# Performer attention with a feed-forward block on one core: the weights' low bits by a 16-bit ScalarE write, and own banks for each half of the first key chunk

## The chip, the core and the metric

The kernel runs on one NeuronCore of a Trainium2 chip: TensorE (PE) for matrix products, VectorE (DVE), ScalarE (ACT), GpSimd (POOL), and SyncE (SP), whose queue issues nearly all transfers. Each engine works through its own instructions in the order in which they were written; an instruction that has to wait holds up all behind it on that engine. PE writes to PSUM, which has eight banks of 512 fp32 values for each of the 128 partitions.

The metric is the device time of one execution in microseconds (us). Before the change three runs gave 965.83, 966.06 and 967.17 us: the median is 966.06 us.

## What is computed

```python
def phi(x):                       # x: (8, 8, 576, 64), omega: (128, 64)
    h = einsum('bhsd,md->bhsm', x, omega) - sum(x * x, -1) / 2
    return exp(h - max(h, -1)) / sqrt(m)
q_p, k_p = phi(q * scale), phi(k * scale)
kv, z = einsum('bhsm,bhsd->bhmd', k_p, v), sum(k_p, axis=2)
num, den = einsum('bhsm,bhmd->bhsd', q_p, kv), einsum('bhsm,bhm->bhs', q_p, z)
x = (num / (den + 1e-6)) as (8, 576, 512)
xn = (x - mean(x)) / sqrt(var(x) + 1e-6) * g_ln
out = x + relu(xn @ w_ch1) @ w_ch2          # 512 -> 2048 -> 512
```

The weights `w_ch1`, `w_ch2` and the vector `g_ln` come as 64-bit floats, the rest as 32-bit.

## The kernel before

**Tiles.** The 8·576 = 4608 rows are cut into 36 chunks of 128, four of them to a tile of 512: nine tiles. The feed-forward block takes a tile through 16 parts f of the hidden layer. Part f of the first layer (`mm1`, L1041 to L1043) is 12 matmuls of 128x512: four slices of the inner dimension, each as high·high, low·high and high·low halves of values that are split in two. Part f of the second layer (`mm2`, L1082 to L1084) is 12 more. Between them `relu` empties the bank: ScalarE writes the high half (L1055), VectorE the low half (L1057).

**Attention** runs between these parts, as visits of PE: keys of a chunk against omega (`gen_k`, L638; the first chunk L629), sums over keys and values (`gen_sums`, L701), queries against omega (`gen_q`, L799; later ones L816, L817), and the quotient's two sides for a chunk (`gen_x`, L882). For keys VectorE takes the negated row maximum (L641) and ScalarE the exponential (L647). For queries a copy leaves PSUM, POOL's all-reduce takes a maximum over partitions (L828), VectorE subtracts it (L833) and ScalarE exponentiates (L836). `gen_x` divides on VectorE (L889, L891, L893, which makes x). A normalised copy xn (L966) is transposed: for the first tile by PE (L1011), ScalarE's copy (L1015) and VectorE's remainder (L1017); for later tiles by a transposing DMA (`gen_flip`): ScalarE splits into 16-bit halves (L983), SP issues (L986), and ScalarE (L354) or VectorE (L356) puts the halves together.

**The first matmuls of the feed-forward block** need x of the first two chunks, so the first tile's keys, values and queries all come ahead of them. Up to then dummy matmuls on a tile named `spin` (L474) fill PE. Eight banks stand for this stage; three pairs of them (0 to 5) are handed out to keys and queries. The first key chunk is worked in two halves (`gen_k_half`, L654): both write into one pair of banks and into columns of one tile of maxima, `mb`, and the pair is given back when both halves are exponentiated.

**Weights** (`gen_w`, L501) come in 32 parts of 512 KB, 64-bit values as pairs of 32-bit words: `r[:, :, 0]` the low word, `r[:, :, 1]` the high word. A part is made into one fp32 value by integer work: the sign bit, the high word scaled as an fp32 number by 2^-112 and shifted left by three, and the upper three bits of the low word below that. Then it is split into a high and a low half (`w[:, 0]`, L354 or L356; `w[:, 1]`, L555 or L549). There are two ways up to the shift: with ScalarE first (L515: low word times 2^-29, written as a 32-bit integer; L517 on VectorE ors in the sign; L360 or L362 scales), or with VectorE first (L523 sign, L527 shift and or). Thirty parts go the first way, two the second. L531 shifts and ors.

**What sets the order.** All instructions are written out by a planner (`Plan`) that keeps its own clock for each engine, takes the ready step with the smallest rank, and knows constants for queues and transfers. `SHIFT` (L1176) is a table that moves the rank of single steps. Different constants and shifts give another order on every engine.

Of the kernel before, what the change touches and what calls it, by code (L numbers as in the profile page):

```python
# [308 lines left out]
def favor_ffn(ctx, tc, kT, kTr, vF, vR, qT, qD, omT, gT, w1, w2, out):  # L309
# [48 lines left out]
    def scaled(eng, out, in_, c):  # L358
        if eng == ACT:
            nc.scalar.activation(out=out, in_=in_, func=AF.Copy, scale=c)  # L360
        else:
            nc.vector.tensor_scalar(out=out, in0=in_, scalar1=c, scalar2=None, op0=ALU.mult)  # L362
# [138 lines left out]
    def gen_w(n, f):  # L501
# [6 lines left out]
            yield wait(*BEFORE)  # L508
        w_turn = yield "get", turn["w"]
        wt = yield "get", n_big  # L510
        eng = yield either(0.58, 0.34)
        t = tile_of(wt, [P, DM], U32)
        sign = 0x80000000
        if eng == ACT:
            nc.scalar.activation(out=t, in_=r[:, :, 0], func=AF.Copy, scale=2.0**-29 * 7.49 / 8)  # L515
            yield dve2(DM)
            nc.vector.scalar_tensor_tensor(  # L517
                out=r[:, :, 0], in0=r[:, :, 1], scalar=sign, in1=t, op0=ALU.bitwise_and, op1=ALU.bitwise_or
            )
            eng = yield either(0.58, 0.34)  # L520
            scaled(eng, f32(r[:, :, 1]), f32(r[:, :, 1]), 2.0**-112)
        else:
            nc.vector.tensor_scalar(out=t, in0=r[:, :, 1], scalar1=sign, scalar2=None, op0=ALU.bitwise_and)  # L523
            eng = yield either(0.58, 0.34)
            scaled(eng, f32(r[:, :, 1]), f32(r[:, :, 1]), 2.0**-112)
            yield dve2(DM)
            nc.vector.scalar_tensor_tensor(  # L527
                out=r[:, :, 0], in0=r[:, :, 0], scalar=29, in1=t, op0=ALU.logical_shift_right, op1=ALU.bitwise_or
            )
        yield dve2(DM)  # L530
        nc.vector.scalar_tensor_tensor(  # L531
            out=t, in0=r[:, :, 1], scalar=3, in1=r[:, :, 0], op0=ALU.logical_shift_left, op1=ALU.bitwise_or
        )
# [66 lines left out]
    def gen_k(b, c, kraw, early, owners, t_v, n_kp, last):  # L600
# [17 lines left out]
        yield wait("om")  # L618

        if not last:  # L620
            t_b = yield "pair", pairs_now()
            pk = two(t_b).rearrange("p s (a b) -> p s a b", b=M)
            left_k = [0, 1]
            for i in range(2):
                yield "run", {PE: 0.5}, 0.03
                for p in range(2 * i, 2 * i + 2):
                    for h in range(2):
                        a = slice(h * D, (h + 1) * D)
                        nc.tensor.matmul(pk[:, h, p], kraw[a, p], om[a], start=True, stop=True)  # L629
# [21 lines left out]
        free(t_mb)  # L651
        done(("kp", b, c))

    def gen_k_half(b, c, i, pk, mb, kp, left_k, t_b, t_mb):  # L654
        cols = slice(2 * i, 2 * i + 2)
        yield dve(4 * M)
        nc.vector.tensor_reduce(
            out=mb.rearrange("p (s a) -> p s a", s=2)[:, :, cols], in_=pk[:, :, cols], axis=AX.X, op=ALU.max, negate=True
        )
        yield us(ACT, 1.0)  # L660
        for s in range(2):
            for p in range(cols.start, cols.stop):
                j = slot(2 * p + s)
                nc.scalar.activation(
                    out=kp[:, j], in_=pk[:, s, p], func=AF.Exp, scale=1.0, bias=mb[:, j : j + 1]
                )
# [312 lines left out]
    def gen_flip(t, i, xn, t_n, xn_turn):  # L979
# [3 lines left out]
        nc.scalar.copy(out=halves, in_=xn.bitcast(U16).rearrange("p (a b) -> p b a", b=2))  # L983
# [252 lines left out]
```

## Time and profile before

| | |
|---|---|
| median of three runs | 966.06 us |
| the profiled execution's own time | 967.0 us |
| its span, first to last instruction | 965.2 us |
| around the span | 1.8 us |
| granted TensorE clock, mean | 1.000 |
| DVE busy | 450.9 us (47%) |
| ACT busy | 406.4 us (42%) |
| POOL busy | 120.4 us (12%) |
| first `mm1` matmul | 34.56 us after the span's start |
| dummy matmuls | 47 |
| moved by DMA | 91.45 MB, 29.6% of 16 engines' span |

Times in the profile are counted from the span's start. A row of the timeline has the start, the length, engine, line, operation, what it writes and reads, and in brackets how long the engine had been idle and what ended that. Matmuls overlap each other, so a row's length is longer than the distance from one start to the next; work on PE, VectorE and ScalarE is counted here by distances between starts. A row of the waits has the total, the number and the longest.

### The profile page before, as it was taken

How to read it: one execution, taken by the hardware profiler on the slowest of the kernel's cores; microseconds unless marked ns; L12 is line 12 of the kernel's file. 1: busy time of each engine (PE TensorE's matmuls, PEld its weight loads, DVE VectorE, ACT ScalarE, POOL GpSimd, SP SyncE). 2: the span in 40 equal slices, each digit the busy share in tenths (PEclk: the TensorE clock that was granted, in tenths of full speed). 3: DMA queues.
4: the chain of work that ended last, by engine and by line, in shares of the span. 5: the costliest groups of instructions: out<-in, count | busy, mean ns of one | idle time of the engine just before them, and what ended most of it. 6: DMA issues, size and time to landing. Idle time of an engine off the chain costs nothing.

```text
span 965.2 us, 15982 instructions
## 1 busy us (share of the span) xinstructions
PE 955.8 (99%) x6731; PEld 787.2 (82%) x6731; DVE 450.9 (47%) x787; ACT 406.4 (42%) x753; POOL 120.4 (12%) x47
## 2 busy tenths in 40 slices
PE   8999999999999999999999999999999999999998
PEld 6877778788888888888888888788888888888886
DVE  6999976245534574344553254535342131113112
ACT  6899874265344543445363234554232121101010
POOL 5012104021010140113011040032010000000000
PEclk9999999999999999999999999999999999999999
DMA  8676364224343243324250213322212020002001
GB/s 299 232 262 229 132 175 124 86 88 131 67 133 98 70 124 104 89 77 100 77 161 16 88 56 91 106 67 77 77 45 77 1 98 1 1 1 87 1 1 44
DMA packets 70584, 91.45 MB, mean 95 GB/s; under 512 B 38000, under 2 KB 38384, under 8 KB 70512
## 3 DMA queue, kind: packets, MB, share of 16 engines
q1 hardware_dynamic: 70368, 90.17, 29.6%
q8 instruction: 53, 0.87, 0.4%
q10 hardware_dynamic: 144, 0.26, 0.1%
q14 instruction: 19, 0.16, 0.1%
HBM read 63.15 MB, written 18.87 MB: 85 GB/s over the span
## 4 chain that ended last, share of the span: by engine, by line
PE 52%; ACT 1%; DMA 1%; DVE 0%; issue 0%; DVEq 0%; ACTq 0%
PE b L1082 8%; PE b L1041 8%; PE b L1084 8%; PE b L1043 8%; PE b L1083 8%; PE b L1042 8%; PE b L882 1%; PE b L701 1%; PE b L638 1%; PE b L816 1%; PE b L817 1%; DMA wide<-wide 1%; ACT wide L354 0%; DVE x L893 0%; ACT quad L809 0%
## 5 line engine op out<-in xcount | busy, mean ns | idle before, releaser
L1057 DVE SCALAR_TENSOR_TENSOR hid<-b,hid 128x512 fp32r<-128x512 f32 x144 | 99.3, 690 | 341.1 <-ACT hid L1055 340.6
L1082 PE MATMUL b<-w,hid 128*128 128x512 f32 x577 | 228.8, 396 | 1.1 <-ACT hid L1055 1.1
L1041 PE MATMUL b<-xnT,w 128*128 128x512 f32 (+1 forms) x584 | 227.0, 389 | 0.7 <-ACT kp L647 0.7
L1042 PE MATMUL b<-xnT,w 128*128 128x512 f32 (+1 forms) x584 | 225.7, 386 | 0.0
L1043 PE MATMUL b<-xnT,w 128*128 128x512 f32 (+1 forms) x584 | 225.6, 386 | 0.0
L1084 PE MATMUL b<-w,hid 128*128 128x512 f32 x577 | 224.8, 390 | 0.0
L1083 PE MATMUL b<-w,hid 128*128 128x512 f32 x577 | 224.6, 389 | 0.0
L1055 ACT ACTIVATE hid<-b 128x512 fp32r<-128x512 f32 x144 | 86.3, 599 | 319.7 <-PE b L1043 319.4
L828 POOL PARTITION_ALL_REDUCE quad<-quad x34 | 114.2, 3388 | 595.5 <-ACT quad L354 360.1
L1082 PEld LDWEIGHTS b<-w,hid 128*128 128x128 f32 x577 | 108.2, 188 | 27.3 <-ACT hid L1055 1.5
L1041 PEld LDWEIGHTS b<-xnT,w 128*128 128x128 f32 x584 | 109.7, 188 | 24.2 <-ACT kp L647 1.7
L1043 PEld LDWEIGHTS b<-xnT,w 128*128 128x128 f32 x584 | 109.7, 188 | 22.3
L1084 PEld LDWEIGHTS b<-w,hid 128*128 128x128 f32 x577 | 108.4, 188 | 23.8 <-DVE hid L1057 0.7
L1042 PEld LDWEIGHTS b<-xnT,w 128*128 128x128 f32 x584 | 109.7, 188 | 22.1 <-DVE w L555 0.4
L1083 PEld LDWEIGHTS b<-w,hid 128*128 128x128 f32 x577 | 108.4, 188 | 21.4
L647 ACT ACTIVATE kp<-b,mb 128x128 f32<-128x128 f32 x256 | 70.1, 395 | 29.6 <-DVE mb L641 29.6
L966 ACT ACTIVATE wide<-x,st 128x512 f32<-128x512 f32 x30 | 21.7, 723 | 84.7 <-DVE x L893 74.5
L833 DVE TENSOR_TENSOR quad<-quad,quad 128x1024 f32<-128x1024 f32 x34 | 53.3, 1575 | 3.5 <-POOL quad L828 3.5
L641 DVE TENSOR_REDUCE mb<-b 128x8 f32<-128x1024 f32 x35 | 41.5, 1218 | 18.0 <-PE b L638 17.5
L836 ACT ACTIVATE quad<-quad 128x1024 f32<-128x1024 f32 x35 | 37.6, 1085 | 26.5 <-DVE quad L833 26.4
L811 DVE TENSOR_TENSOR quad<-quad,quad 64x1024 fp32r<-64x1024 f32 x28 | 35.8, 1288 | 24.1 <-ACT quad L809 24.0
L354 ACT COPY wide<-wide 128x1024 uint16<-128x1024 uint16 x22 | 29.9, 1360 | 28.1 <-DMA wide<-wide 28.0
(100 smaller groups left out, 769.1 us busy)
## 6 DMA issues: line engine op xcount, KB each, us to landing
w<-w SPq DMA_DIRECT2D x32, 512.0 KB, 6.4
quad<-qD SPq DMA_DIRECT2D x28, 512.0 KB, 4.6
away<-x SPq DMA_DIRECT2D x36, 256.0 KB, 2.5
x<-away SPq DMA_DIRECT2D x36, 256.0 KB, 3.8
out<-x SPq DMA_DIRECT2D x35, 256.0 KB, 2.2
v<-vF SPq DMA_DIRECT2D x28, 260.0 KB, 3.5
wide<-kT SPq DMA_DIRECT2D x28, 256.0 KB, 3.4
wide<-qT SPq DMA_DIRECT2D x8, 256.0 KB, 4.7
```

Of the source, the lines that this page charges most:

```text
L641: nc.vector.tensor_reduce(out=mb.rearrange("p (s a) -> p s a", s=2), in_=pk, axis=AX.X, op=ALU.max, negate=True)
L647: nc.scalar.activation(out=kp[:, j], in_=pk[:, s, j % 4], func=AF.Exp, scale=1.0, bias=mb[:, j : j + 1])
L828: nc.gpsimd.partition_all_reduce(mx.rearrange("p a b -> p (a b)"), qc.rearrange("p a b -> p (a b)"), P, bass_isa.ReduceOp.max)
L833: nc.vector.tensor_tensor(out=qc, in0=qc, in1=mx, op=ALU.subtract)
L1041: nc.tensor.matmul(ph[:, ts], w[:, 0, cs], xnT[:, 0, k, ts], start=k + i0 == 0, stop=False)
L1042: nc.tensor.matmul(ph[:, ts], w[:, 1, cs], xnT[:, 0, k, ts], start=False, stop=False)
L1043: nc.tensor.matmul(ph[:, ts], w[:, 0, cs], xnT[:, 1, k, ts], start=False, stop=k == NK - 1 and i1 == TC)
L1055: nc.scalar.activation(out=hl[:, 0], in_=ph, func=AF.Relu)
L1057: nc.vector.scalar_tensor_tensor(out=hl[:, 1], in0=ph, scalar=0.0, in1=f32(hl[:, 0]), op0=ALU.max, op1=ALU.subtract)
L1082: nc.tensor.matmul(accs[i][:, c], hl[:, 0, cs], w[:, 0, c], start=(f == 0), stop=False)
L1083: nc.tensor.matmul(accs[i][:, c], hl[:, 0, cs], w[:, 1, c], start=False, stop=False)
L1084: nc.tensor.matmul(accs[i][:, c], hl[:, 1, cs], w[:, 0, c], start=False, stop=f == NF - 1 and c == parts[-1])
```

## The change

Four things change. `gen_w` has one way only: VectorE writes the sign bit into `t` (L515 now), ScalarE writes the low word's three bits as a 16-bit number into the lower half of each 32-bit value of `t` (L518), the scaling stays on either engine, and one instruction (L522) shifts, ors and finishes `t`. The first key chunk's halves get a pair of banks and a tile of maxima each, and each gives them back by itself. The planner's one constant for the time of a transfer is split by kind, a transposing DMA costs it 2.0 instead of 0.9, and 48 ranks are moved.

```diff
-    ISSUE, FLIGHT, QUEUE, SLOW = 0.47, 1.8, 8, 5.0
+    ISSUE, QUEUE, SLOW = 0.47, 8, 5.5
+    FLIGHT = {"load": 2.4, "flip": 0.75, "store": 1.35}
...
-                self.dma_at = max(self.dma_at, start + Plan.FLIGHT) + cost * (1.55 if self.dma_at < Plan.SLOW else 1.0)
+                kind = part.want[2] if len(part.want) > 2 else "load"
+                self.dma_at = max(self.dma_at, start + Plan.FLIGHT[kind]) + cost * (1.55 if self.dma_at < Plan.SLOW else 1.0)
...
         wt = yield "get", n_big
+        t = tile_of(wt, [P, DM], U32)
+        yield "run", {DVE: 0.34}, "two"
+        nc.vector.tensor_scalar(out=t, in0=r[:, :, 1], scalar1=0x80000000, scalar2=None, op0=ALU.bitwise_and)
+        yield us(ACT, 0.67)
+        low = t.bitcast(U16).rearrange("p (a b) -> p a b", b=2)[:, :, 0]
+        nc.scalar.activation(out=low, in_=r[:, :, 0], func=AF.Copy, scale=2.0**-29 * 7.49 / 8)
         eng = yield either(0.58, 0.34)
-        t = tile_of(wt, [P, DM], U32)
-        sign = 0x80000000
-        if eng == ACT:
...
-        else:
...
+        scaled(eng, f32(r[:, :, 1]), f32(r[:, :, 1]), 2.0**-112)
         yield dve2(DM)
         nc.vector.scalar_tensor_tensor(
-            out=t, in0=r[:, :, 1], scalar=3, in1=r[:, :, 0], op0=ALU.logical_shift_left, op1=ALU.bitwise_or
+            out=t, in0=r[:, :, 1], scalar=3, in1=t, op0=ALU.logical_shift_left, op1=ALU.bitwise_or
         )
...
-            t_b = yield "pair", pairs_now()
-            pk = two(t_b).rearrange("p s (a b) -> p s a b", b=M)
             left_k = [0, 1]
-            for i in range(2):
+            t_m0 = yield "get", n_mb
+            t_b0 = yield "pair", pairs_now()
+            t_b1 = yield "pair", pairs_now()
+            for i, t_b, t_mi in ((0, t_b0, t_m0), (1, t_b1, t_mb)):
                 yield "run", {PE: 0.5}, 0.03
-                for p in range(2 * i, 2 * i + 2):
+                pk = two(t_b, 2 * M).rearrange("p s (a b) -> p s a b", b=M)
+                for p in range(2):
...
-                        nc.tensor.matmul(pk[:, h, p], kraw[a, p], om[a], start=True, stop=True)
-                plan.add(rank, gen_k_half(b, c, i, pk, mb, kp, left_k, t_b, t_mb))
+                        nc.tensor.matmul(pk[:, h, p], kraw[a, 2 * i + p], om[a], start=True, stop=True)
+                plan.add(rank, gen_k_half(b, c, i, pk, kp, left_k, t_b, t_mi))
...
+        free(*t_b)
+        free(t_mi)
         left_k.remove(i)
         if not left_k:
-            free(*t_b)
-            free(t_mb)
             done(("kp", b, c))
...
-        yield "run", {SP: 0.9}, "flip"
+        yield "run", {SP: 2.0}, "flip"
...
-SHIFT = {('gen_k', 0, 0): -17, ('gen_k', 0, 2): -2, ...}
+SHIFT = {('gen_k', 0, 0): -10, ('gen_k', 0, 1): -10, ('gen_k', 0, 3): -1, ...}
```

The order on ScalarE at the start, before. `kp0`, `kp1`, `w2_15`, `w2_13` and `w1_15` take exponentials of key chunks, `mb` their maxima, the `quad` rows belong to queries, `w2_00` and the tile `wide4` to a weight part:

```order
L664 ACTIVATE kp0_118<-b_74,mb0_119 128x128 x8
L354 COPY quad1_174<-b_74 128x1024
L647 ACTIVATE kp1_130<-b_74,mb1_131 128x128 x4
L647 ACTIVATE w2_150_152<-b_74,mb2_153 128x128 x4
L647 ACTIVATE kp1_130<-b_74,mb1_131 128x128 x4
L647 ACTIVATE w2_150_152<-b_74,mb2_153 128x128 x4
L836 ACTIVATE quad0_163<-quad0_163 128x1024
L515 ACTIVATE wide4_297<-w2_00_191 128x512
```

The same place of the change:

```order
L656 ACTIVATE kp0_118<-b_74,mb2_150 128x128 x4
L656 ACTIVATE kp0_118<-b_74,mb0_159 128x128 x4
L356 COPY quad0_189<-b_74 128x1024
L640 ACTIVATE kp1_127<-b_74,mb1_128 128x128 x8
L640 ACTIVATE w2_150_167<-b_74,mb2_168 128x128 x4
L518 ACTIVATE wide4_154<-w1_00_152 128x512
L640 ACTIVATE w2_150_167<-b_74,mb2_168 128x128 x4
L640 ACTIVATE w2_140_184<-b_74,mb0_185 128x128 x4
L356 COPY quad4_291<-b_74 128x1024
```

The halves of the first chunk now have a tile of maxima each, the first weight's 16-bit write stands between exponentials, and a second query's copy has come to ScalarE.

On VectorE, before, the last twelve rows down to the first x (L893); ahead of them stand the third query's subtraction (L833), two memsets, L517 and L523. `w2_00`, `w1_00`, `w1_10` and the `wide` tiles are weight parts, `dn` a chunk's denominators:

```order
L362 TENSOR_SCALAR w2_00_191<-w2_00_191 128x512
L362 TENSOR_SCALAR w1_00_196<-w1_00_196 128x512
L531 SCALAR_TENSOR_TENSOR wide4_297<-w2_00_191 128x512
L527 SCALAR_TENSOR_TENSOR w1_00_196<-w1_00_196,wide5_381 128x512
L523 TENSOR_SCALAR wide6_423<-w1_10_210 128x512
L531 SCALAR_TENSOR_TENSOR wide5_381<-w1_00_196 128x512
L555 TENSOR_TENSOR w2_00_421<-wide4_297,w2_00_421 128x512
L889 TENSOR_SCALAR dn0_406<-b_74 128x8
L539 TENSOR_TENSOR wide5_381<-wide5_381,g_sb_83 128x512
L891 RECIPROCAL dn0_406<-dn0_406 128x8
L527 SCALAR_TENSOR_TENSOR w1_10_210<-w1_10_210,wide6_423 128x512
L893 SCALAR_TENSOR_TENSOR x0_405,st0_404<-b_74,dn0_406 128x512
```

And in the change, from the same subtraction (L826 now) to the first x (L886):

```order
L826 TENSOR_TENSOR quad4_291<-quad4_291,w2_120_309 128x1024
L530 TENSOR_TENSOR wide4_154<-wide4_154,g_sb_83 128x512
L515 TENSOR_SCALAR wide5_210<-w2_00_208 128x512
L358 CAST w1_00_434<-wide4_154 128x512
L515 TENSOR_SCALAR wide6_236<-w1_10_234 128x512
L546 TENSOR_TENSOR w1_00_434<-wide4_154,w1_00_434 128x512
L882 TENSOR_SCALAR dn0_410<-b_74 128x8
L364 TENSOR_SCALAR w2_00_208<-w2_00_208 128x512
L884 RECIPROCAL dn0_410<-dn0_410 128x8
L515 TENSOR_SCALAR wide7_439<-w1_20_254 128x512
L886 SCALAR_TENSOR_TENSOR x0_409,st0_408<-b_74,dn0_410 128x512
```

Eleven instructions on weights stood between the subtraction and the first x, seven of them of the long forms (SCALAR_TENSOR_TENSOR, TENSOR_TENSOR); now there are seven, two of them long.

The third place is on ScalarE, at the first chunk of the third tile: normalised (L966), split into 16-bit halves (L983), sent through the transposing DMA, and put together again (L354, 128x2x512). Before:

```order
L966 ACTIVATE wide0_2006<-x0_1939,st2_1938 128x512
L983 COPY wide5_2009<-wide0_2006 128x1024
L809 CAST quad4_2003<-quad2_1964 128x1024
L354 COPY wide5_2034<-wide0_2032 128x2x512
L647 ACTIVATE kp0_2016<-b_74,mb0_2017 128x128 x4
L1055 ACTIVATE hid0_2066<-b_74 128x512
```

The same chunk in the change:

```order
L959 ACTIVATE wide0_1874<-x2_1772,st2_1771 128x512
L802 CAST quad4_1864<-quad0_1821 128x1024
L976 COPY wide6_1886<-wide0_1874 128x1024
L829 ACTIVATE quad2_1768<-quad2_1768 128x1024
L1048 ACTIVATE hid0_1915<-b_74 128x512
L1048 ACTIVATE hid1_1934<-b_74 128x512
L356 COPY wide6_1911<-wide0_1909 128x2x512
L640 ACTIVATE kp1_1870<-b_74,mb1_1871 128x128 x4
```

Between the split and the copy stood one instruction; now there are three, two of them the `relu` copies (L1048) that PE's second layer waits for. Of all 32 such copies ScalarE makes 30, where it made 22; VectorE makes the others.

On PE the first tile's four transposes now all stand ahead of the first `mm1` matmul, where the fourth stood behind six of them; `mm1` of part 3 comes after two parts of `mm2` instead of three; and the stretches of keys, sums and quotients that interrupt the feed-forward block are 49 instead of 46. On SP the first weight part is fetched ahead of the key chunks 3 and 4.

More of the change, by code (lines that the diff above doesn't have):

```diff
@@ L289, in run @@
             part.eng = eng
-            part.lat = part.want[2] if len(part.want) > 2 and part.want[2] not in ("two", "flip") else Plan.LAT[eng]
+            part.lat = part.want[2] if len(part.want) > 2 and part.want[2] not in ("two", "flip", "store") else Plan.LAT[eng]
             if eng == SP:
@@ L347, in us, with dma @@
         return "run", {eng: t}
-    def dma(n):
-        return "run", {SP: n * 4e-6 / 0.4}
+    def dma(n, *kind):
+        return "run", {SP: n * 4e-6 / 0.4}, *kind
     def copy(eng, out, in_):
@@ L510, in gen_w @@
         wt = yield "get", n_big
-        eng = yield either(0.58, 0.34)
-        t = tile_of(wt, [P, DM], U32)
-        sign = 0x80000000
-        if eng == ACT:
[L515 to L521, printed above, removed]
-        else:
[L523 to L529, printed above, removed]
+        t = tile_of(wt, [P, DM], U32)
[4 more added lines that the diff above has]
+        nc.scalar.activation(out=low, in_=r[:, :, 0], func=AF.Copy, scale=2.0**-29 * 7.49 / 8)
+        eng = yield either(0.58, 0.34)
+        scaled(eng, f32(r[:, :, 1]), f32(r[:, :, 1]), 2.0**-112)
         yield dve2(DM)
         nc.vector.scalar_tensor_tensor(
-            out=t, in0=r[:, :, 1], scalar=3, in1=r[:, :, 0], op0=ALU.logical_shift_left, op1=ALU.bitwise_or
+            out=t, in0=r[:, :, 1], scalar=3, in1=t, op0=ALU.logical_shift_left, op1=ALU.bitwise_or
         )
@@ L652, in gen_k, with gen_k_half @@
         done(("kp", b, c))
-    def gen_k_half(b, c, i, pk, mb, kp, left_k, t_b, t_mb):
-        cols = slice(2 * i, 2 * i + 2)
+    def gen_k_half(b, c, i, pk, kp, left_k, t_b, t_mi):
+        mi = tile_of(t_mi, [P, H])
         yield dve(4 * M)
         nc.vector.tensor_reduce(
-            out=mb.rearrange("p (s a) -> p s a", s=2)[:, :, cols], in_=pk[:, :, cols], axis=AX.X, op=ALU.max, negate=True
+            out=mi[:, 0:4].rearrange("p (s a) -> p s a", s=2), in_=pk, axis=AX.X, op=ALU.max, negate=True
         )
@@ L661, in gen_k_half @@
         for s in range(2):
-            for p in range(cols.start, cols.stop):
-                j = slot(2 * p + s)
+            for p in range(2):
                 nc.scalar.activation(
-                    out=kp[:, j], in_=pk[:, s, p], func=AF.Exp, scale=1.0, bias=mb[:, j : j + 1]
-                )
+                    out=kp[:, slot(4 * i + 2 * p + s)], in_=pk[:, s, p], func=AF.Exp, scale=1.0,
+                    bias=mi[:, 2 * s + p : 2 * s + p + 1],
+                )
+        free(*t_b)
+        free(t_mi)
         left_k.remove(i)
         if not left_k:
-            free(*t_b)
-            free(t_mb)
             done(("kp", b, c))
@@ L907, in gen_spill @@
         away[c] = dram.tile([P, DM], F32, tag=f"away{c}", name=f"away{c}", bufs=1)
-        yield dma(P * DM)
+        yield dma(P * DM, "store")
         nc.sync.dma_start(away[c], x)
@@ L1109, in store @@
     def store(c, t_x, x, p, last):
-        yield dma(P * (p.stop - p.start))
+        yield dma(P * (p.stop - p.start), "store")
         nc.sync.dma_start(out[c * P : (c + 1) * P, p], x[:, p])
@@ L1173, in favor_ffn @@
     plan.run()
-SHIFT = {('gen_k', 0, 0): -17, ('gen_k', 0, 2): -2, ('gen_k', 2, 0): 23, ('gen_k', 2, 1): 24, ('gen_k', 2, 4): -14, ('gen_q', 1): -20, ('gen_q', 12): 38, ('gen_q', 3): -5, ('gen_q', 5): 34, ('gen_q', 8): 11, ('gen_v', 0, 0): 21, ('gen_v', 0, 3): -4, ('gen_var', 6): -29, ('gen_w', 1, 12): -2, ('gen_w', 1, 13): 5, ('gen_w', 1, 3): 1, ('gen_w', 1, 4): -1, ('gen_w', 2, 0): -4, ('gen_w', 2, 13): 29, ('gen_w', 2, 2): 1, ('gen_w', 2, 3): -17, ('gen_x', 11): 35, ('gen_x', 2): 4, ('gen_x', 3): 5, ('gen_x', 6): 52}
+SHIFT = {('gen_k', 0, 0): -10, ('gen_k', 0, 1): -10, ('gen_k', 0, 3): -1, ('gen_k', 1, 1): -19, ('gen_k', 1, 2): 4, ('gen_k', 2, 4): -48, ('gen_q', 0): 4, ('gen_q', 1): -8, ('gen_q', 12): 45, ('gen_q', 17): 101, ('gen_q', 2): -1, ('gen_q', 3): 8, ('gen_q', 4): -27, ('gen_sums', 1, 0): 106, ('gen_sums', 3, 0): 13, ('gen_sums', 3, 1): -49, ('gen_sums', 3, 2): -50, ('gen_sums', 5, 2): 32, ('gen_v', 0, 1): 7, ('gen_v', 1, 0): -8, ('gen_v', 1, 1): 57, ('gen_v', 1, 3): 62, ('gen_v', 7, 1): -11, ('gen_w', 1, 0): -15, ('gen_w', 1, 12): 10, ('gen_w', 1, 13): 7, ('gen_w', 1, 14): 6, ('gen_w', 1, 15): 2, ('gen_w', 1, 8): -54, ('gen_w', 1, 9): 5, ('gen_w', 2, 10): 6, ('gen_w', 2, 11): 6, ('gen_w', 2, 12): 36, ('gen_w', 2, 14): 10, ('gen_w', 2, 15): 21, ('gen_w', 2, 3): -2, ('gen_w', 2, 5): 1, ('gen_w', 2, 6): 2, ('gen_w', 2, 7): 6, ('gen_w', 2, 8): 6, ('gen_w', 2, 9): 5, ('gen_x', 10): 39, ('gen_x', 12): 53, ('gen_x', 14): 42, ('gen_x', 16): 54, ('gen_x', 3): -64, ('gen_x', 30): -33, ('gen_x', 6): 5}
 LINE = 16
```

## The prediction

> **What bounds the kernel now.** I read the page first, then stretches, PE's waits, and timelines of the start. Part 1 of the page, and a table by stretches (columns: stretch, length, busy time of PE, PEld, DVE, ACT and POOL with instructions in brackets, clock, DMA share, GB/s):
>
> ```profile
> PE 955.8 (99%) x6731; PEld 787.2 (82%) x6731; DVE 450.9 (47%) x787; ACT 406.4 (42%) x753; POOL 120.4 (12%) x47
> ```
>
> ```profile
> 10.00:15.00 5.00, 4.97 (x73) 3.68 (x73) 3.31 (x8) 3.40 (x11) 4.74 (x2) 1.00 1.05 409
> ...
> 20.00:34.50 14.50, 14.10 (x298) 11.93 (x295) 14.39 (x38) 12.94 (x28) 0.05 (x1) 1.00 0.33 117
> 34.50:60.00 25.50, 25.50 (x207) 21.12 (x207) 25.50 (x46) 22.84 (x49) 3.22 (x1) 1.00 0.79 280
> ...
> 150.00:965.20 815.20, 809.59 (x5345) 670.23 (x5343) 316.64 (x541) 283.44 (x496) 88.95 (x27) 1.00 0.24 73
> ```
>
> VectorE is full from 20 to 60 us, DMA at 10 to 15 us, and yet PE behind 34.5 us hardly idles, at full clock. What PE's waits come to:
>
> ```profile
> PE b L638 <- ACT kp L664: 1.3, 1, 1.3
> ...
> PE b L1082 <- ACT hid L1055: 1.1, 1, 1.1
> ...
> PE b L799 <- DVE x L893: 0.5, 1, 0.5
> ```
>
> So the end is set by the moment at which PE's feed-forward stream begins, by the work in it, and by a few waits. VectorE work saved behind that moment is worth only the waits that it ends; saved ahead of it, it counts in full. PE and VectorE at that moment:
>
> ```profile
> 34.56 0.36 PE L1041 MATMUL b<-xnT,w 128*128 128x256 f32 x1
> ...
> 35.35 0.64 PE L1011 MATMUL b<-ident,wide 128*128 128x128 f32 x4
> 35.75 0.36 PE L1041 MATMUL b<-xnT,w 128*128 128x256 f32 x1
> ```
>
> ```profile
> 8.27 0.69 DVE L657 TENSOR_REDUCE mb<-b 128x4 f32<-128x512 f32 x1 [1.21 <-ACT kp L664]
> ...
> 20.17 1.21 DVE L833 TENSOR_TENSOR quad<-quad,quad 128x1024 f32<-128x1024 f32 x1
> 21.30 1.22 DVE L833 TENSOR_TENSOR quad<-quad,w 128x1024 f32<-128x1024 f32 x1
> ...
> 23.31 0.42 DVE L523 TENSOR_SCALAR wide<-w 128x512 uint32<-128x512 uint32 x1
> 23.65 0.78 DVE L362 TENSOR_SCALAR w<-w 128x512 f32<-128x512 f32 x2
> 24.33 0.69 DVE L531 SCALAR_TENSOR_TENSOR wide<-w 128x512 uint32<-128x512 uint32 x1
> 24.93 0.69 DVE L527 SCALAR_TENSOR_TENSOR w<-w,wide 128x512 uint32<-128x512 uint32 x1
> ...
> 33.79 0.69 DVE L1017 TENSOR_TENSOR xnT<-b,xnT 128x512 fp32r<-128x512 f32 x1
> ```
>
> The first matmul at 34.56 waits for the second L1017, which stands at the end of VectorE's full queue. From start to start: 1.13 us for 1024 values (20.17 to 21.30), 0.60 for a long form (24.33 to 24.93), 0.34 for a TENSOR_SCALAR between SBUF tiles.
>
> **The weights' form.** Thirty parts lose L517 (0.60) and gain a sign (0.34), two lose 0.34 + 0.60 + 0.60 for 0.34 + 0.60: VectorE saves 30 x 0.26 + 2 x 0.60 = 9.0 us. Nearly all lies behind 34.5 us and under PE, worth nothing by itself. ScalarE's write with 16-bit output is not in the trace. Its bounds are the 16-bit copies of 1024, halved for 512, and beside them stands the 32-bit form in ScalarE's timeline:
>
> ```profile
> L983 ACT COPY wide<-wide 128x1024 uint16<-128x1024 uint16 x32 | 32.9, 1043 | 3.5 <-issue 2.0 <-DVE xnT L1000 1.1
> L354 ACT COPY wide<-wide 128x1024 uint16<-128x1024 uint16 x22 | 29.9, 1360 | 28.1 <-DMA wide<-wide 28.0
> ```
>
> ```profile
> 43.40 1.24 ACT L515 ACTIVATE wide<-w 128x512 uint32<-128x512 uint32 x2 [0.86 <-DVE w L555]
> 44.55 1.89 ACT L360 ACTIVATE w<-w 128x512 f32<-128x512 f32 x3
> ```
>
> That is 0.52 to 0.68 us; two of the 32-bit form, nearest in kind, take 1.15 from start to start. I take 0.57. Only one stands in ScalarE's queue ahead of the last keys, so the bounds move the start by -0.05 to +0.1.
>
> **The start on ScalarE**, before, with the first chunk's products on PE:
>
> ```profile
> 4.24 2.08 PE L629 MATMUL b<-om,w 64*128 64x128 f32 x16
> ```
>
> ```profile
> 7.09 1.14 ACT L664 ACTIVATE kp<-b,mb 128x128 f32<-128x128 f32 x4 [4.65 <-DVE mb L657]
> 8.99 1.14 ACT L664 ACTIVATE kp<-b,mb 128x128 f32<-128x128 f32 x4 [0.76 <-DVE mb L657]
> 10.01 1.03 ACT L354 COPY quad<-b 128x1024 f32<-128x1024 f32 x1
> 12.64 1.14 ACT L647 ACTIVATE kp<-b,mb 128x128 f32<-128x128 f32 x4 [1.60 <-DVE mb L641]
> ...
> 22.46 2.24 ACT L836 ACTIVATE quad<-quad 128x1024 f32<-128x1024 f32 x2
> 24.59 0.59 ACT L354 COPY kv<-b 128x520 f32<-128x520 f32 x1
> ```
>
> The second half's maximum (8.27) waits 1.21 for the first half's exponentials, PE's next keys (L638) 1.3 us for the second half's. With own banks and maxima both waits go, the next keys' products no longer come last, and the idle 0.76 + 1.60 = 2.36 closes up, because ScalarE then has work in hand throughout. The first maximum need not wait for the second half's products either, half of the 2.08 us of L629; I take 0.9. The order gives ScalarE one query copy (1.03) and one scaling (0.58) more ahead of the kv copy and one exponential of a query (1.06, half of 22.46 to 24.59) fewer: +0.55. A gap of about 0.2 stays at the third chunk's maximum. The kv copy moves from 24.59 to 24.59 - 2.36 - 0.9 + 0.55 + 0.2 = 22.1.
>
> **Then VectorE.** With 0.5 for the kv copy and 1.1 for 32 products, PE has the first quotient ready at 23.7, but VectorE has its queue. Its last subtraction (20.17 plus a change of -0.6, as it waits for the first weight's scaling) starts at 20.6 instead of 21.30. From there to the second xnT remainder the order has 1 instruction of 1.13, 13 of 0.60 to 0.61, 6 of 0.34 and 8 small ones (0.76 in all): 11.8, where the rows above show 33.79 + 0.60 - 21.30 = 13.1. So it ends at 32.4 instead of 34.39, and PE starts at 32.5: **-2.1 us**. The four transposes then stand ahead, hidden under VectorE: **-0.4** (35.35 to 35.75). From 0, if the keys come no sooner, to -3.5, if VectorE were never held by ScalarE.
>
> **Late weights.** PE comes to part 3 of `mm1` sooner: 48 half-width matmuls at 0.12 (5.8), three parts at 2.7 and a query visit (1.2): 32.5 + 15.1 = 47.6. VectorE has seven signs (2.4), 19 long forms (11.4) and 2.3 of others up to the last step of that weight: 32.3 + 16.1 = 48.4, and PE waits 0.8, of which 0.2 is spent already on the first `relu`: **+0.6**, between 0 and +1.5. Before, a third part of `mm2` and two visits for keys stood between, and PE's waits name no weight.
>
> **Stretches.** Three more interruptions by keys, sums or quotients. The chain of work shows one alone and one in the middle of others:
>
> ```profile
> 531.66 0.94 PE b L882 x32
> ...
> 562.32 1.08 PE b L882 x32
> 563.40 0.43 PE b L1041
> ```
>
> Alone it is 1.08 - 0.94 = 0.14 longer, and the first matmul behind it takes 0.43 instead of 0.23: 0.34 each, **+1.0**.
>
> **Two waits.** The 1.1 us at L1082 has this cause:
>
> ```profile
> 171.17 1.35 ACT L354 COPY wide<-wide 128x1024 uint16<-128x1024 uint16 x1 [5.79 <-DMA wide<-wide]
> ...
> 173.39 0.62 ACT L1055 ACTIVATE hid<-b 128x512 fp32r<-128x512 f32 x1
> ```
>
> ScalarE waits 5.79 us for a transposed chunk with the `relu` that PE needs behind it. In the change two `relu` copies stand between split and copy, so I let it go, with the slow first matmul: **-1.2**. L799's 0.5 us waits for x in VectorE's full queue; VectorE runs freer by then: **-0.5**. The other waits I leave as they are.
>
> Sum: -2.1 - 0.4 + 0.6 + 1.0 - 1.2 - 0.5 = -2.6. The profiled execution took 967.0 (span 965.2 and 1.8 around it), so 964.4 by its measure; it lies 0.9 above the median 966.06, so the forecast for a median is **963.4**.
>
> **A lock of two engines.** The new signs are of a kind that can be held up while POOL works:
>
> ```profile
> 89.80 6.89 POOL L828 PARTITION_ALL_REDUCE quad<-quad  x2 [33.10 <-ACT quad L354]
> ```
>
> ```profile
> 90.16 1.65 DVE L938 TENSOR_SCALAR st<-st 128x4 f32<-128x4 f32 x1
> 91.72 0.68 DVE L555 TENSOR_TENSOR w<-wide,w 128x512 fp32r<-128x512 f32 x1
> ```
>
> Four values took 1.65 us until 91.81, that is until 2.0 us after the reduce began. The first query's reduce can begin near 9.5, behind the copy of 1.03 that follows the second half's exponentials at 8.3; the first weight's sign comes some 2 us later, behind its transfer, so by this row it is free, and the sum holds. [...] The L555 at 91.72, in the middle of the reduce, at its usual pace, does not bear out a lock held to the end for every form.
>
> **Rivals.**
> 1. *The lock is held for a whole reduce.* Then the sign waits to 12.7, the write to 13.1 instead of 12.4, and all of ScalarE's start with it: +0.7, 964.1; with a second hit among the later signs, up to 1.3 more while weights are late: 965.4. Against it is the row at 91.72. Chance 0.08.
> 2. *The first chunk's halves still wait for each other,* or the keys' transfers, now behind 512 KB of weights, come too late.
>
> ```profile
> 8.43 0.98 SPq L593 DMA_DIRECT2D w<-vR  x2
> ```
>
> ```profile
> w<-vR SPq DMA_DIRECT2D x2, 260.0 KB, 5.2
> ```
>
> The last values are issued at about 9.1 and land 5.2 later, at 14.3. At the 409 GB/s of the stretch above, 512 KB less the 256 KB of one query put behind are 0.6 us more: 14.9, where VectorE would reach their memsets at 14.2, with 0.9 us in hand at the last keys' exponentials. If they come 1.5 us later than that, or the halves wait, the start gains 0.5 instead of 2.1: 965.0; with the late weights at their upper bound 965.9. Chance 0.25.
> 3. *More waits end.* The trace has some 3 us of other waits behind the start. If half go too and no weight is late: 963.4 - 1.6 - 0.6 = 961.2. Chance 0.20.
> 4. *Slower: transposed chunks hold up `relu`.* ScalarE gets 30 of 32 copies instead of 22. Each holds up what stands behind it; in the row at 171.17 a wait of 5.79 cost PE 1.2, so waiting for more than some 4.6 us decides. Four such copies in tiles 2 to 8 cost +4.8, and the old one back +1.2: 963.4 + 6.0 = 969.4; two, with the old one, 967.0. For it: eight copies more; against it: by the order 6.6 instructions on average stand from split to copy instead of 4.5. Chance 0.14.
>
> The forecast has 0.33, by its own from 962.4 to 964.6. **The range** reaches from 961.0 to 967.0, which leaves half of rival 4 and the rest of rival 3 out. 0.2% of the median are 1.9 us, about what a measurement of this kernel tells from no change; below 964.1 lie most of the forecast's case, rival 3 and some of rival 1: faster 0.54. Rival 2 and the rest are within 0.2%: 0.33. Slower is rival 4's upper part: 0.13.
>
> **What would show it.** After the change the first chunk's two maxima should follow each other with no wait for ScalarE; the kv copy should start near 22, the first `mm1` matmul near 32.5; PE should wait some 0.6 us at part 3 of `mm1`; the 1.1 us of L1082's successor should be gone. VectorE should have room from some 55 us on, without any gain in time from it. The forecast is wrong if the first matmul starts after 34, or if PE's waits behind it grow by more than 2 us.

## The result, and the profile after

The changed kernel takes 975.52 us (median of four runs, 975.06 to 977.05) against 966.57 for the kernel before beside it: the ratio is 1.009, with a 95% interval from 1.0077 to 1.0104. It is slower by 0.9%; the forecast was 963.4 us and faster. In the change's line numbers the first `mm1` line is L1034, `mm2` is L1075 to L1077, `relu` L1048 (ScalarE) and L1050 (VectorE), the all-reduce L821, its subtraction L826, the low half of a later query L804, queries on PE L809 and L810, quotients L875, sums L694, and the two halves of a transposed chunk L356 or L358 and L993.

Part 1 of the page, and the waits of PE:

```profile
PE 957.1 (98%) x6732; PEld 787.3 (81%) x6732; DVE 456.5 (47%) x796; ACT 407.0 (42%) x744; POOL 120.1 (12%) x47
```

```profile
PE b L875 <- DVE hid L1050: 3.3, 2, 2.4
PE b L809 <- DVE quad L804: 3.3, 5, 1.2
PE b L694 <- DVE hid L1050: 2.7, 2, 2.4
...
PE b L1035 <- DVE w L546: 0.2, 1, 0.2
```

No engine has more work than before; VectorE is busy for 5.6 us more, but its held instructions, counted below, alone take 9.9 us more. PE waits for VectorE instead: twice 2.4 us for a `relu`, up to 1.2 us for the low halves of queries. The 1.1 us for L1082's `relu` and the 0.5 us for L799 are gone. The profiled executions split as follows (worked out from PE's instructions and the span):

| us | before | after |
|---|---|---|
| first `mm1` matmul | 34.56 | 34.38 |
| from there to PE's end | 926.94 | 934.34 |
| behind PE's end | 3.71 | 4.55 |
| span | 965.21 | 973.27 |

So the start gained 0.2 instead of the 2.1 that I forecast, and 7.4 us were lost in the feed-forward stream. PE's idle time behind its first `mm1` matmul grew by nearly as much, from 2.8 to 10.1 us.

**One of the two long waits.** Timelines of VectorE, ScalarE, POOL and PE after the change, at the end of the second tile:

```profile
142.23 2.11 DVE L358 CAST xnT<-wide 128x512 fp32r<-128x512 f32 x2
144.26 2.37 DVE L993 TENSOR_TENSOR xnT<-wide,xnT 128x512 fp32r<-128x512 f32 x1
146.56 0.68 DVE L1050 SCALAR_TENSOR_TENSOR hid<-b,hid 128x512 fp32r<-128x512 f32 x1
```

```profile
142.99 0.58 ACT L1048 ACTIVATE hid<-b 128x512 fp32r<-128x512 f32 x1
```

```profile
139.77 7.65 POOL L821 PARTITION_ALL_REDUCE quad<-quad  x2 [1.73 <-DVE quad L804]
```

```profile
147.29 0.92 PE L875 MATMUL b<-kv,quad 128*64 128x65 f32 x24 [2.38 <-DVE hid L1050]
```

ScalarE had written its half of `hid` at 143.6. VectorE could read the bank only at 146.56, because two instructions ahead of it, L358 and L993, took 2.11 (two of 0.42 otherwise) and 2.37 (0.68 otherwise) beside two all-reduces of POOL (the second began at 143.97 and took 3.45). PE's next visit needs that bank.

**The chain behind L809.** The same engines at the start of the fourth tile's normalisation, where five instructions on four values (`gen_rs`) stand ahead of a query's low half:

```profile
337.10 1.70 DVE L939 TENSOR_TENSOR st<-st 128x4 f32<-128x4 f32 x1 [0.40 <-ACT st L937]
338.84 0.16 DVE L941 TENSOR_TENSOR st<-st 128x4 f32<-128x4 f32 x1
339.03 1.11 DVE L943 TENSOR_SCALAR st<-st 128x4 f32<-128x4 f32 x1
...
340.37 1.22 DVE L804 TENSOR_TENSOR quad<-quad,quad 64x1024 fp32r<-64x1024 f32 x1
```

```profile
336.89 3.22 POOL L821 PARTITION_ALL_REDUCE quad<-quad  x1 [26.09 <-ACT st L935]
```

```profile
341.74 0.47 PE L809 MATMUL b<-quad,om_hi 128*128 128x512 f32 x1 [1.19 <-DVE quad L804]
```

The first of these steps takes 1.70 us for four values and ends 1.91 after the reduce began (337.10 + 1.70 - 336.89). L941, also with two inputs from SBUF, begins 1.95 after it and takes 0.16, its usual time. L943, with one such input, begins 2.14 after it, takes 1.11 and ends at 3.25. PE waits 1.19 us behind them.

What a form with one input pays hangs on when it begins. Another step of that kind, further on in the same trace:

```profile
500.46 1.52 DVE L931 TENSOR_SCALAR st<-st 128x4 f32<-128x4 f32 x1
```

```profile
500.06 3.22 POOL L821 PARTITION_ALL_REDUCE quad<-quad  x1 [42.88 <-ACT quad L356]
```

It begins 0.40 after its reduce and ends at 1.92, not at 3.25; so does L931 at 605.52, and the prediction's row at 90.16 ended at 2.01.

**How much is held in all.** I call a VectorE instruction held when it is at least 0.25 us longer than its kind usually is: 19 with 23.0 us of excess before, 26 with 32.9 us after, and every one of them overlaps an all-reduce. Groups of VectorE by form (total us, mean ns), before:

```profile
L833 DVE TENSOR_TENSOR quad<-quad,quad 128x1024 f32<-128x1024 f32 x34 | 53.3, 1575 | 3.5 <-POOL quad L828 3.5
L1000 DVE TENSOR_TENSOR xnT<-wide,xnT 128x512 fp32r<-128x512 f32 x32 | 19.9, 682 | 0.0
...
L938 DVE TENSOR_SCALAR st<-st 128x4 f32<-128x4 f32 x9 | 3.0, 334 | 0.2
```

and after:

```profile
L826 DVE TENSOR_TENSOR quad<-quad,quad 128x1024 f32<-128x1024 f32 x34 | 47.8, 1410 | 11.8 <-POOL quad L821 11.7
...
L993 DVE TENSOR_TENSOR xnT<-wide,xnT 128x512 fp32r<-128x512 f32 x32 | 23.5, 790 | 0.0
...
L931 DVE TENSOR_SCALAR st<-st 128x4 f32<-128x4 f32 x9 | 4.3, 481 | 0.3
```

Before, most of the held time fell on the queries' own subtraction (1575 ns instead of 1218), which nobody on PE awaits at once, and none on the low halves of transposed chunks (682). After, the subtraction is held less and those low halves and the steps on four values more.

The rows of the subtraction show a second price of a reduce: VectorE stands idle until it is done, 11.7 us in all after the change and 3.5 before. This did not make the two long waits. From 134.88 to the `relu` at 146.56, and over the same stretch at the third tile's end, VectorE is never idle for more than 0.14 us. One idle time of 1.95 us, at 513.56, does stand ahead of a PE wait of 0.91 at 517.15.

### The profile page after: what moved, and what is told of

It reads as the page before. It is cut to its first block, busy times and chain, and to the rows that moved or that the text cites. A ratio compares the mean times of both kernels' runs of the same rounds, so it can differ in the third digit from the quotient of the medians.

```text
span 973.3 us, 16026 instructions
## 1 busy us (share of the span) xinstructions
PE 957.1 (98%) x6732; PEld 787.3 (81%) x6732; DVE 456.5 (47%) x796; ACT 407.0 (42%) x744; POOL 120.1 (12%) x47
## 5 line engine op out<-in xcount | busy, mean ns | idle before, releaser
L1050 DVE SCALAR_TENSOR_TENSOR hid<-b,hid 128x512 fp32r<-128x512 f32 x144 | 99.4, 691 | 367.1 <-ACT hid L1048 366.6
L1075 PE MATMUL b<-w,hid 128*128 128x512 f32 x577 | 228.7, 396 | 0.0
L1034 PE MATMUL b<-xnT,w 128*128 128x512 f32 (+1 forms) x584 | 227.3, 389 | 0.0
L1077 PE MATMUL b<-w,hid 128*128 128x512 f32 x577 | 224.8, 390 | 0.4 <-DVE hid L1050 0.4
L1048 ACT ACTIVATE hid<-b 128x512 fp32r<-128x512 f32 x144 | 86.0, 597 | 321.3 <-PE b L1036 320.6
L821 POOL PARTITION_ALL_REDUCE quad<-quad x34 | 114.0, 3374 | 605.8 <-ACT quad L356 348.6
L1034 PEld LDWEIGHTS b<-xnT,w 128*128 128x128 f32 x584 | 109.7, 188 | 24.2 <-ACT w L356 0.8
L1075 PEld LDWEIGHTS b<-w,hid 128*128 128x128 f32 x577 | 108.3, 188 | 25.1 <-issue 0.8
L1077 PEld LDWEIGHTS b<-w,hid 128*128 128x128 f32 x577 | 108.4, 188 | 23.8 <-DVE hid L1050 1.0
L826 DVE TENSOR_TENSOR quad<-quad,quad 128x1024 f32<-128x1024 f32 x34 | 47.8, 1410 | 11.8 <-POOL quad L821 11.7
L829 ACT ACTIVATE quad<-quad 128x1024 f32<-128x1024 f32 x35 | 37.4, 1073 | 29.5 <-DVE quad L826 29.5
L959 ACT ACTIVATE wide<-x,st 128x512 f32<-128x512 f32 x26 | 18.7, 723 | 70.3 <-DVE x L886 62.1
L804 DVE TENSOR_TENSOR quad<-quad,quad 64x1024 fp32r<-64x1024 f32 x28 | 36.0, 1296 | 20.5 <-ACT quad L802 20.2
L356 ACT COPY wide<-wide 128x1024 uint16<-128x1024 uint16 x30 | 40.5, 1361 | 11.3 <-DMA wide<-wide 11.1
```

What stands on the lines that cost most here:

```text
L821: nc.gpsimd.partition_all_reduce(mx.rearrange("p a b -> p (a b)"), qc.rearrange("p a b -> p (a b)"), P, bass_isa.ReduceOp.max)
L826: nc.vector.tensor_tensor(out=qc, in0=qc, in1=mx, op=ALU.subtract)
L1034: nc.tensor.matmul(ph[:, ts], w[:, 0, cs], xnT[:, 0, k, ts], start=k + i0 == 0, stop=False)
L1048: nc.scalar.activation(out=hl[:, 0], in_=ph, func=AF.Relu)
L1050: nc.vector.scalar_tensor_tensor(out=hl[:, 1], in0=ph, scalar=0.0, in1=f32(hl[:, 0]), op0=ALU.max, op1=ALU.subtract)
L1075: nc.tensor.matmul(accs[i][:, c], hl[:, 0, cs], w[:, 0, c], start=(f == 0), stop=False)
```

## The experiments

Three theories stood against each other. **A**: POOL's all-reduces hold VectorE's instructions, and the new order puts them where PE needs VectorE next. **B**, my rival 4: ScalarE's additional copies of transposed chunks hold up `relu`. **C**: the new instructions cost more than I took. The first two runs keep the order and shorten the reduces:

```diff
-            mx.rearrange("p a b -> p (a b)"), qc.rearrange("p a b -> p (a b)"), P, bass_isa.ReduceOp.max
+            mx.rearrange("p a b -> p (a b)")[:, 0:8], qc.rearrange("p a b -> p (a b)")[:, 0:8], P, bass_isa.ReduceOp.max
...
-        nc.vector.tensor_tensor(out=qc, in0=qc, in1=mx, op=ALU.subtract)
+        nc.vector.tensor_tensor(out=qc, in0=qc, in1=mx[:, 0:1, 0:1].to_broadcast([P, 2, 4 * P]), op=ALU.subtract)
```

> The changed kernel with the same order of instructions, but each of GpSimd's all-reduces works on 8 of 1024 columns, and the subtraction behind it takes one column's maximum for all: most of the query maximum is left out, so that GpSimd is busy for a fraction of the time. Theory A (GpSimd's reduces hold up VectorE where PE needs it next): the stalls of 2.3 us at 144.5 and 264.5, of 1.1 at 340 and 0.9 at 516 go, and some of the smaller ones; 975.5 becomes 965 to 968. Theory B (ScalarE's additional copies of transposed chunks hold up relu, my rival 4): nothing in that depends on GpSimd, 974 to 976. Theory C (the new instructions themselves are slower than taken): 974 to 976 as well.

> The kernel before with the same shortening of GpSimd's all-reduces (most of the query maximum left out), order unchanged. Theory A: its long VectorE instructions beside a reduce (23.0 us in all, against 32.9 after the change) mostly cost PE nothing, so it gains 0 to 3 us: 963.5 to 966.5; the distance to the shortened changed kernel then falls from 9 to under 3 us. Theories B and C: the distance stays near 9 us.

Measured: the changed kernel with short reduces 964.59 us (ratio to the kernel before 0.9977, 0.9962 to 0.9993), the kernel before with short reduces 964.67 (0.9979, 0.9969 to 0.9990). The change loses 10.9 us of its time, the kernel before 2.0, and the distance of 9 us is gone. No VectorE instruction is 0.25 us longer than usual in either. Groups by form of the shortened changed kernel:

```profile
L826 DVE TENSOR_TENSOR quad<-quad,quad 128x1024 f32<-128x1024 f32 x34 | 41.1, 1218 | 3.2 <-POOL quad L821 3.0
...
L993 DVE TENSOR_TENSOR xnT<-wide,xnT 128x512 fp32r<-128x512 f32 x32 | 20.1, 684 | 0.0
...
L931 DVE TENSOR_SCALAR st<-st 128x4 f32<-128x4 f32 x9 | 1.5, 170 | 0.3
```

So what cost the 9 us hangs on the reduces, as in A; the result came 0.4 us below A's range. B and C fall as causes: ScalarE's 30 copies and all 32 new weight parts are still there. Short reduces also end most of VectorE's idle time behind them (3.0 us are left), so these two runs alone don't part the hold from the idle time; at the two long waits the trace does.

The next two separate the code from the constants and ranks: the code of the change with the planner's constants and `SHIFT` of before, and the reverse.

```diff
-    ISSUE, QUEUE, SLOW = 0.47, 8, 5.5
-    FLIGHT = {"load": 2.4, "flip": 0.75, "store": 1.35}
+    ISSUE, QUEUE, SLOW = 0.47, 8, 5.0
+    FLIGHT = {"load": 1.8, "flip": 1.8, "store": 1.8}
...
-        yield "run", {SP: 2.0}, "flip"
+        yield "run", {SP: 0.9}, "flip"
...
-SHIFT = {('gen_k', 0, 0): -10, ('gen_k', 0, 1): -10, ...}
+SHIFT = {('gen_k', 0, 0): -17, ('gen_k', 0, 2): -2, ...}
```

> The changed code (weights' form, own banks) with the planner's constants and the 48 ranks of before. Theory A (what costs is where the new order puts reduces and tile boundaries): the code alone costs nothing, 963 to 968, since its order lies nearer to that of before. Theory C (the instructions cost): 973 or more, as the 30 weight parts are all there.

> The code of before (two ways of the weights' form, shared banks for the halves) with the planner's constants and the ranks of the change. Theory A: the order carries the cost, 970 to 977. Theory C: the code carries it, 964 to 968. The ranks were made for other instructions, so some of the order differs from both kernels, and a time in between says only that both have a part.

Measured: 971.0 us (ratio 1.0041) and 977.99 (1.0116). The table and constants carry the cost even with the old code, 1 us beyond A's range; 1.6 us of it are a later first `mm1` matmul (36.12). The code alone came out 3 us above what A allowed, so neither theory has it whole: old ranks on new instructions give a third order, with 5.9 us of PE waits of its own behind its first `mm1` matmul. The table's order has the same long wait, for the same `relu`:

```profile
PE b L703 <- DVE hid L1059: 2.6, 2, 2.4
PE b L818 <- DVE quad L813: 2.5, 4, 1.2
```

Then the places, and my failed step at the start:

```diff
+        cut = 8 if c in (8, 9, 10, 12, 13, 14) else 8 * P
```

(with the columns `0:cut`, and the broadcast where `cut` is 8), and by itself

```diff
-        for h in range(H):
+        for h in range(H // 2 if o == 0 and g in (1, 2) else H):
```

> The changed kernel in which only six of GpSimd's 36 all-reduces are shortened to 8 columns, those of queries 8, 9, 10, 12, 13 and 14 (most of these queries' maximum is left out); they stand at 134 to 147 and at 254 to 267 us, beside the work that makes the next tile's transposed inputs. Theory A as narrowed by the first runs (the cost sits at few places, where what is held is the work in front of relu): the two waits of 2.4 us at L875 and L694 and the shorter ones ahead of them go, 975.5 becomes 968 to 970.5, more than half of the 11 us that shortening all of them gave. If the cost is spread evenly over the reduces, 6 of 36 give about 1.8 us: 973.5 to 974.

> The changed kernel, in which the sums of keys and values of the first batch take four of eight heads in two of their chunks (half of these chunks' sums is left out), so that PE has some 1.1 us less to do between 13.6 and 17.8 us. Theory D (the start did not come sooner because the fourth query's products on PE, and so its maximum at 19.05 on VectorE, come behind a full PE): that maximum moves to 18.0, and the first mm1 matmul from 34.4 to about 33.4. Rival (ScalarE, which has no idle time from 6.9 to 22.7 us, sets it): the copy of kv stays near 23.1 and the first mm1 matmul between 34.2 and 34.5.

Six short reduces of 36 give 968.22 us (1.0013, 1.0003 to 1.0022): 7.3 us of the 10.9. Two thirds of the cost sit at two tile boundaries, and not evenly in the reduces.

For the start, rows of VectorE, PE and ScalarE after the change; L745 is the fourth query's row maximum, L743 its products:

```profile
16.83 1.23 DVE L634 TENSOR_REDUCE mb<-b 128x8 f32<-128x1024 f32 x1
19.05 1.23 DVE L745 TENSOR_REDUCE w<-b 128x8 f32<-128x1024 f32 x1 [0.99 <-ACT quad L829]
20.19 1.22 DVE L826 TENSOR_TENSOR quad<-quad,quad 128x1024 f32<-128x1024 f32 x1
21.32 0.69 DVE L522 SCALAR_TENSOR_TENSOR wide<-w,wide 128x512 uint32<-128x512 uint32 x1
21.93 1.22 DVE L826 TENSOR_TENSOR quad<-quad,w 128x1024 f32<-128x1024 f32 x1
```

```profile
17.74 1.16 PE L743 MATMUL b<-om,wide 64*128 64x128 f32 x16
```

```profile
23.08 0.59 ACT L356 COPY kv<-b 128x520 f32<-128x520 f32 x1 [0.31 <-PE b L694]
```

and of the run with half the sums:

```profile
17.89 1.21 DVE L745 TENSOR_REDUCE w<-b 128x8 f32<-128x1024 f32 x1
```

```profile
33.20 0.36 PE L1034 MATMUL b<-xnT,w 128*128 128x256 f32 x1
```

With 1.1 us less on PE the maximum comes 1.16 sooner and the first `mm1` matmul 1.18 sooner: the start hung on PE's queue of products, theory D. (The trace names L829 as the releaser at 19.05, since it ended at 19.04. In the run with half the sums L745 starts at 17.89, while L829 runs until 18.3; so L745 doesn't wait for it, but for L743, which ended at 18.9 in the change.) The whole run took 976.39, no less than the change; the last section shows where the 1.2 us went.

In the last six runs the planner is told of the hold: a form with two inputs from SBUF ("two") is held until 1.91 us after a reduce's start, one with a single SBUF input ("one") until 3.25. It had released every form at 1.9 and taken the five steps on four values to be free. The 3.25 fits one-input steps that begin late, such as L943 at 339.03; for those that begin early, such as L931 at 500.46, it is 1.3 us too long, so this picture is better than the old one, but not exact.

```diff
-    LOCK = 1.9
+    HELD = {"two": 1.91, "one": 3.25}
...
-            if e == DVE and part.want[-1] == "two" and self.lock[0] <= start < self.lock[1]:
-                start = self.lock[1]
+            if e == DVE and str(part.want[-1]) in Plan.HELD and self.lock <= start < self.lock + Plan.HELD[part.want[-1]]:
+                start = self.lock + Plan.HELD[part.want[-1]]
...
-        return "run", {ACT: a, DVE: d}, "two"
+        return "run", {ACT: a, DVE: d}, "one"
...
-        yield us(DVE, 0.085)
+        yield "run", {DVE: 0.085}, "one"
```

(`self.lock` is the reduce's start; the `gen_rs` steps are "one", "two", "two", "one", "two".) The first run keeps the ranks of before; the others have ranks found by a search under this planner.

> The changed code with the ranks and constants of before, as in the third run (971.0), but the planner is told what the traces show of a reduce: it holds a VectorE instruction with two inputs from SBUF until 1.91 us after its start and one with one such input until 3.25, the five steps on four values among them, which it took to be free. Theory A: fewer instructions that PE waits for are held; 966 to 969. If the order is luck and the planner's picture of the hold doesn't matter: 965 to 976, with as much of VectorE's time held as before (21 us).

> The changed code with the planner told of the holds and with ranks searched anew under it. Theory A: PE's waits for relu and for query splits behind a reduce go almost wholly; the time comes near that of the two kernels with shortened reduces (964.6), 962 to 966. If the planner's picture is still wrong in what matters, some of the waits of 1 us and more stay: 967 to 975.

> As the run before, from another search of the ranks, to see whether one good order is luck: theory A 962 to 967; otherwise anywhere up to 975.

> The code of before (two ways of the weights' form, shared banks) with the planner told of the holds and ranks searched anew for it. Theory A: like the changed code with the same planner, 962 to 967, since the code itself then matters little; if the new code is worth something by itself (2 us at the start, as I had forecast), it lies 1 to 3 us above the changed code.

Measured: 969.81, 966.32 (ratio 0.9997, 0.9984 to 1.0009), 971.96 and 968.38 us. They lie 0.8, 0.3, 5.0 and 1.4 above their ranges by A: the hold alone doesn't make an order good. What was left was another wait. ScalarE and PE in `held_new`:

```profile
236.54 1.05 ACT L802 CAST quad<-quad 128x1024 fp32r<-128x1024 f32 x1 [1.75 <-DMA quad<-qD]
237.50 1.04 ACT L976 COPY wide<-wide 128x1024 uint16<-128x1024 uint16 x1
...
238.55 1.03 ACT L802 CAST quad<-quad 128x1024 fp32r<-128x1024 f32 x1
239.49 0.58 ACT L1048 ACTIVATE hid<-b 128x512 fp32r<-128x512 f32 x1
```

```profile
240.12 0.50 PE L1075 MATMUL b<-w,hid 128*128 128x512 f32 x1 [0.78 <-ACT hid L1048]
```

A query that lands late puts three copies of 1 us in front of `relu`: rival 4's mechanism, though with a query's transfer at its head, and `held_new2` has two waits of PE for this `relu`, 1.6 us in all. These four runs used the constants of before, in which a load is taken to fly 1.8 us. The last two have those of the change (2.4):

> The changed kernel with its own constants for the queues (a load is taken to fly 2.4 us, where the kernels before it in these runs used 1.8), the planner told of the holds, and ranks searched anew. What is left in the best order so far are two waits of 0.8 us for relu at 240, where ScalarE stands behind a query that lands 1.75 us after the instruction ahead of it. Theory A with that: those go, 962 to 965.5, at or below the kernel before by 0.1 to 0.4%. If the constants of the change are the worse ones, other waits of that kind come in their place: 966 to 972.

> As the run before, with ranks from another search: 962 to 966 by theory A; up to 972 if orders that the planner takes for good still differ by luck on the chip.

Measured: 963.30 us (962.42 to 964.65; ratio 0.9962, 0.9949 to 0.9976) and 963.46 (0.9966, 0.9954 to 0.9979). Two searches agree, and both beat both kernels: the kernel before by 0.4%, the change by 1.3%. What part of this the corrected planner has is not shown: the searches also moved far more ranks (126 and 113 entries in `SHIFT`, where the change has 48), and no run has such a search under the old planner. Waits of PE and groups by form of `held_after`:

```profile
PE b L1034 <- DVE x L886: 1.2, 1, 1.2
...
PE b L1077 <- DVE hid L1050: 0.2, 1, 0.2
```

```profile
L826 DVE TENSOR_TENSOR quad<-quad,quad 128x1024 f32<-128x1024 f32 x34 | 54.6, 1610 | 7.1 <-POOL quad L821 7.0
L993 DVE TENSOR_TENSOR xnT<-wide,xnT 128x512 fp32r<-128x512 f32 x32 | 19.9, 686 | 0.0
...
L931 DVE TENSOR_SCALAR st<-st 128x4 f32<-128x4 f32 x9 | 1.5, 168 | 0.2
```

VectorE is still held for 20.0 us, but 13.3 of them fall on the queries' subtraction. Its first `mm1` matmul even starts later, at 35.51, and the stream behind takes 922.29 us instead of 926.94. In `held_after2` the two are 33.96 and 924.38, and 13.9 us are held. The time lies in the stream, not at the start.

## Why the prediction was wrong

- **The other waits I leave as they are.** This step failed, and with it the sign. I counted the instructions that moved, their durations and two known waits, but not where the moved reduces fall. PE's idle time behind the start, which this step left at what it was, grew by 7.3 us. Six reduces in two places cost 7.3 us, all of them 9 more after the change than before (10.9 against 2.0). I had the sign of it in hand: the four values that took 1.65 us beside a reduce.
- **Rival 1, the lock.** I asked only whether the new signs are held, at the start, and until the reduce ends. The lock was there, but the instructions that it hurt were old ones, and it made most of the 9 us, where I gave it 0.7 to 2.0. The first sign was held as well (1.01 us instead of 0.42), with no effect: with short reduces the first matmul starts at the same 34.38.
- **The start on ScalarE.** The two maxima follow each other, as forecast, and ScalarE's gaps close. The first maximum came 0.22 sooner instead of 0.9 (6.14 after 6.36), and the copy of kv waits 0.31 for PE's sums: it starts at 23.08 instead of 22.1. The 16-bit write took 0.64 from start to start (13.13 to 13.77), within its bounds.
- **Then VectorE, -2.1.** The 11.8 us from the last subtraction to the end were nearly right (12.0, 21.93 to 33.94). That it starts at 20.6 was wrong: the fourth query's maximum comes at 19.05 as before (19.04), behind a full PE, and a weight's step (L522) stands in between now. I followed ScalarE and VectorE there and not PE's own queue. Measured: -0.18. The four transposes do stand ahead of the stream, as forecast (-0.4).
- **Late weights, +0.6**: 0.2, in the place forecast. **Two waits, -1.2 and -0.5**: both gone. **Stretches, +1.0**: not borne out. PE has two more interruptions, and with short reduces the stream takes 925.21 us after the change and 923.93 before, 1.3 more; but PE's waits in it are 2.4 against 1.0, which is all of it. The 0.4 of the transposes has left the stream, so up to some 0.3 us may remain for the interruptions.
- **Rival 4** is not what made the change slow, since the time came back with ScalarE's copies left in place. A late transfer did hold up `relu` in `held_new`, a query's and not a transposed chunk's: PE waited 0.78 us at 240.12.
- **Behind PE's end** the change takes 0.84 us more, for which the sum has no term; with short reduces 0.49 of it stay. No run isolates the cause.

Which forms are held can be read from the traces. After the change eight `relu` low halves (L1050), which read PSUM and SBUF, began within 1.8 us of a reduce's start and took 0.69 us as always. The one-input step that began 2.14 us into a reduce (L943 at 339.03) ended at 3.25, when the reduce had ended at 3.22; the one that began 0.40 into it (L931 at 500.46) ended at 1.92 of 3.22 us. Steps with two inputs from SBUF on four values ended at 1.91 or, begun later, took their usual 0.16.

What stays open: how much the new weight form and the own banks are worth by themselves. The one order of the old code under the new planner (968.38) had the older constants, so it doesn't settle that. Nor is it shown how much of the last two runs' gain comes from the corrected planner, and how much from new ranks as such.

## What to carry to other kernels

An engine's stall must be charged to what waits behind the stalled instruction: shortening the reduces gave 2 us in an order with 23 us of held VectorE work, and 11 in one with 33. Where a planner sets the order, compare its idea of each shared resource with the trace, down to instructions on four values, before adding work or searching ranks: with the hold told to the planner and ranks searched anew under it, the same code went from 0.9% slower to 0.4% faster. And before crediting a gain at the start, follow every queue that feeds the last link, PE's too.

## What the runs showed of the hardware

The reduces are longer in turn where they begin inside a subtraction: the one at 139.77 began 0.22 us behind the start of a subtraction of 1.23 (L826 at 139.55) and took 4.29 us instead of 3.22. Three more began so after the change, inside the L826 at 259.56, 341.62 and 509.23, and took 4.39, 4.18 and 4.05 us.

In two runs PE's granted clock was lower behind a wait of 2.4 us. Stretches (length, busy time of PE, PEld, DVE, ACT, POOL, granted clock, DMA share, GB/s) behind the wait of 2.4 us at the third tile's end, in the change

```profile
268.00:270.00 2.00, 2.00 (x76) 2.00 (x74) 2.00 (x3) 0.57 (x1) 0.00 (x0) 1.00 0.00 0
```

and in the run with half the sums:

```profile
266.00:268.00 2.00, 1.88 (x50) 1.88 (x52) 2.00 (x5) 0.00 (x0) 0.25 (x1) 0.79 0.00 0
268.00:270.00 2.00, 2.00 (x44) 2.00 (x42) 1.00 (x1) 0.97 (x2) 0.00 (x0) 0.50 0.11 16
270.00:272.00 2.00, 2.00 (x20) 1.67 (x17) 1.23 (x3) 0.58 (x1) 0.00 (x0) 0.85 0.43 128
```

Behind the same wait the clock stayed at 1.00 in one run and showed means of 0.79, 0.50 and 0.85 over three stretches of 2 us in the other. Taken as time at 0.50 these are some 3.4 us, (1 - 0.79) x 2 x 2 + 2 + (1 - 0.85) x 2 x 2, worth 1.7 us, which is my estimate. That is the 1.2 us that the earlier start had gained, and more. The run with the ranks of the change and the old code has a clock of 0.50 from 270 to 272 us, also behind its one wait of 2.4 us. The clock did not fall each time: of the five waits of 2.4 us in these three runs it was below 1.00 behind two, and from 144 to 152 us, around the wait that ends at 147.29 in the change, it was 1.00. The changed kernel's run with the longest time, 977.05 us, had a mean clock of 0.997 where the other three had 0.999.
